# A gated block of local attention and GeGLU on one core: the instruction order is written by a list scheduler, the first token block goes in two halves, and TensorE gets warm-up matmuls

## The chip, the cores and the metric

The kernel runs on one core of a Trainium2 chip. Its time is that of one execution on the device in microseconds, and the median of several executions is what kernels are compared by. A core has five engines that run side by side, each through its own list of instructions in the order of that list: TensorE (PE, matmuls), VectorE (DVE), ScalarE (ACT), GpSimd (POOL) and SyncE (SP), which here only issues DMAs. An instruction that waits for another engine holds up everything behind it in its own list.

## The reference

The input x is 2048 tokens of 512 features, in bfloat16. After a layer norm without weights two branches start: an attention with 32 heads of 16 features, in which each token looks at itself and at seven earlier tokens two apart (offsets 0, 2, ..., 14), and a GeGLU feed-forward with 1792 hidden features. The output is x plus the attention branch times the silu of the feed-forward branch.

```python
def _A_ref(x, wqkv, wo):
    B, S, D = x.shape
    H = 32; Dh = D // H
    W, dil = 8, 2
    qkv = (lambda x, *d: x.transpose(*d))((x @ wqkv).reshape(B, S, 3, H, Dh), 2, 0, 3, 1, 4)
    q, k, v = qkv[0], qkv[1], qkv[2]
    scale = Dh ** -0.5
    pos = jnp.arange(S)
    off = jnp.arange(W) * dil
    idx = pos[:, None] - off[None, :]
    mask = idx >= 0
    ...
    logits = jnp.einsum("bhsd,bhswd->bhsw", q, kg) * scale
    logits = jnp.where(mask[None, None, :, :], logits, -1e9)
    attn = _softmax(logits, axis=-1)
    o = jnp.einsum("bhsw,bhswd->bhsd", attn, vg)
    return (lambda x, *d: x.transpose(*d))(o, 0, 2, 1, 3).reshape(B, S, D) @ wo
...
def _B_ref(x, w_gate, w_up, w_down):
    g = jnp.einsum("bsd,df->bsf", x, w_gate)
    u = jnp.einsum("bsd,df->bsf", x, w_up)
    h = _gelu(g) * u
    return jnp.einsum("bsf,fd->bsd", h, w_down)

x = A_x
xn = _layernorm(x, axis=-1)
s = _A_ref(xn, A_wqkv, A_wo)
g = _silu(_B_ref(xn, B_w_gate, B_w_up, B_w_down))
return x + s * g
```

## The kernel before

Tokens are taken in four blocks of 512 (`NJ`, index `j`), each of four tiles of 128 (`TPB`). All of x, the normalised and transposed x (`xnT`), the keys (`k_sb`) and all weights lie in on-chip memory. The weights come in one DMA each; `wqkv_sb` shares its place with the hidden activations `hT`.

*Layer norm.* `ln_stats` (from L194) has VectorE compute mean and variance of the four tiles of a block, and GpSimd `1/sqrt(var + eps)` by an add and a power (L200, L203). `ln_norm` (L210) normalises a tile on VectorE; `ln_transpose` transposes it by four TensorE matmuls (L224) and VectorE copies the result out of PSUM into `xnT` (L225).

*QKV.* `qkv_group` makes 128 of the 1536 output features for a block by four matmuls over 512 tokens (L416), and ScalarE copies them from PSUM: queries (L428), keys (L430), and values (L435), which are also written to DRAM (`vT_dram`, L436). There are twelve such groups a block.

*Attention* of a block (`queue_scores`, `queue_values`). VectorE multiplies the queries by shifted windows of the keys (L247, eight products of 128x2048); TensorE adds them up by head with a 0/1 matrix into `L_ps` (L260, 16 matmuls for each half of the window offsets); ScalarE takes the exponential (L273); TensorE sums over the window (L291), VectorE takes the reciprocal (L299), TensorE spreads it back (L307) and ScalarE copies it (L315). VectorE then normalises and multiplies the weights by shifted values (L342, eight products), which `load_values` has fetched from `vT_dram` in two halves of four DMAs (L408); TensorE adds the products up into `O_ps` (L357, 16 matmuls a half) and ScalarE copies them out (L364).

*Feed-forward.* `ffn_pair` makes 128 hidden features: four matmuls for the gate (L450), gelu on ScalarE (L459), four for up (L465), and VectorE's product into `hT` (L475). There are 14 pairs a block. `out_tile` makes 128 tokens of output: the attention's projection (`s_ps`, four matmuls, L484), the down projection (`y_ps`, 14 matmuls, L495), silu on ScalarE (L505), two multiply-adds on VectorE (L509, L510) and the store (L512).

*PSUM.* Four buffers (`psf`) serve the groups of QKV, gate, up, s and y in turn; two (`psa`) the transposes, `L_ps`, sums and spreads; one (`pso`) `O_ps`.

*What sets the order.* It is written out when the kernel is built: the loops at the end emit QKV for blocks 0 to 3, then for each block its 14 pairs and its four output tiles. The layer norm of block j+1 is emitted at fixed places among the groups of block j. Attention is put between by rough clocks of three engines (`clk`): after each group `pump_dve` emits products from one queue in order as long as they fit before a given time, `pump_pe` and `pump_act` emit reductions and exponentials whose time has come. ScalarE's table loads (for gelu, exp, silu; plain copies need none) are in no clock. The first four tiles of x and all later x come on SyncE's queue, `wqkv` on ScalarE's; the other weights follow on SyncE's after the values of blocks 0, 1 and 2.

## Time and profile before

| | us |
|---|---|
| median of three executions | 259.02 (258.78 to 261.68) |
| profiled execution, its own time | 258.46 |
| its span, first to last instruction | 256.4 |
| TensorE busy | 228.1 (89%) |
| VectorE busy | 158.8 (62%) |
| ScalarE busy | 107.2 (42%) |
| GpSimd busy | 11.2 (4%) |
| granted TensorE clock, mean | 0.996 |

The span is the part of the execution between the first and the last instruction of the kernel; the rest of the time lies around it. Busy time of TensorE is the union of its matmuls from start to (modelled) end; matmuls overlap, so the mean duration of one (379 ns) is longer than the distance from one to the next. In the views below a line stands for the instructions of one source line; "idle before" or an entry in square brackets is the time in which the engine stood idle just before, and what released it.

### The profile page before, as it was taken

The numbers are of one execution on the slowest core, as the hardware profiler recorded it, in microseconds if no ns is written. First come the engines' busy times: TensorE is split into PE (matmuls) and PEld (weight loads), VectorE is DVE, ScalarE is ACT, GpSimd is POOL, SyncE is SP. The second block draws the span as 40 slices with busy tenths as digits, with TensorE's granted clock in tenths as the row PEclk, the third lists the DMA queues.
The fourth block names the chain that finished last, engine by engine and source line by source line (L and its number), as shares of the span: only waits on it lengthen the run. The fifth ranks groups of instructions, "written<-read, shape, count | busy, mean of one in ns | idle before, by whom it ended". The sixth has DMA issues, their size and how long they took to land.

```text
span 256.4 us, 3342 instructions
## 1 busy us (share of the span) xinstructions
PE 228.1 (89%) x1296; PEld 100.0 (39%) x1296; DVE 158.8 (62%) x228; ACT 107.2 (42%) x157; POOL 11.2 (4%) x46
## 2 busy tenths in 40 slices
PE   0069979798999998999779999999999999999993
PEld 0034433333344443434234444444444444444441
DVE  2464758789987988999869742239953134344131
ACT  2006644545576477444664433143444105334110
POOL 6104010100000000000000000000000000000000
PEclk9999999999999999999999999999999999999998
DMA  6900289995778600377003400100000010000001
GB/s 211 348 14 0 83 296 210 293 295 140 216 243 210 115 3 0 82 163 147 26 1 86 84 0 3 41 23 18 3 0 1 20 43 20 0 0 3 20 20 41
DMA packets 20511, 22.58 MB, mean 88 GB/s; under 512 B 1296, under 2 KB 19472, under 8 KB 20496
## 3 DMA queue, kind: packets, MB, share of 16 engines
q1 hardware_dynamic: 18912, 20.80, 31.1%
q10 hardware_dynamic: 1584, 1.57, 2.0%
q8 instruction: 10, 0.16, 0.3%
q14 instruction: 5, 0.04, 0.1%
HBM read 18.17 MB, written 4.19 MB: 87 GB/s over the span
## 4 chain that ended last, share of the span: by engine, by line
PE 77%; DVE 13%; ACT 3%; DMA 2%; POOL 1%; issue 1%; SPq 0%; POOLq 0%; ACTq 0%
PE y_ps L495 19%; PE g_ps L450 18%; PE u_ps L465 18%; PE qkv_ps L416 8%; PE s_ps L484 6%; DVE prod L247 5%; PE O_ps L357 3%; PE tr_ps L224 3%; DVE stats L196 2%; DMA x_sb<-in_A_x_dram 2%; DVE xnT L225 2%; PE L_ps L260 2%; DVE xn_t L210 2%; POOL rstd L203 1%; ACT L273 1%
## 5 line engine op out<-in xcount | busy, mean ns | idle before, releaser
L465 PE MATMUL u_ps<-xnT,wu_sb 128*128 128x512 bf16 x224 | 57.5, 379 | 0.0
L450 PE MATMUL g_ps<-xnT,wg_sb 128*128 128x512 bf16 x224 | 57.5, 379 | 0.0
L475 DVE TENSOR_TENSOR hT<-gl,u_ps 128x512 bf16<-128x512 bf16 x56 | 38.2, 684 | 30.8 <-PE u_ps L465 24.7
L459 ACT ACTIVATE gl<-g_ps 128x512 bf16<-128x512 f32 x56 | 33.2, 597 | 45.8 <-PE g_ps L450 45.5
L495 PE MATMUL y_ps<-wd_sb,hT 128*128 128x512 bf16 x224 | 51.0, 379 | 0.0
L416 PE MATMUL qkv_ps<-xnT,wqkv_sb 128*128 128x512 bf16 x192 | 45.7, 386 | 0.5 <-DVE xnT L225 0.5
L342 DVE TENSOR_TENSOR pv<-attn,v_arr 128x2048 bf16<-128x2048 bf16 x32 | 38.3, 1218 | 0.9 <-PE O_ps L357 0.8
L247 DVE TENSOR_TENSOR prod<-q_sb,k_sb 128x2048 bf16<-128x2048 bf16 x32 | 37.9, 1216 | 0.0
L509 DVE TENSOR_TENSOR sg<-sil,s_ps 128x512 bf16<-128x512 bf16 x16 | 11.0, 686 | 37.1 <-ACT sil L505 37.1
L495 PEld LDWEIGHTS <-hT 128*128 128x128 bf16 x224 | 21.9, 98 | 26.4
L465 PEld LDWEIGHTS <-wu_sb 128*128 128x128 bf16 x224 | 21.5, 98 | 26.7 <-issue 1.6
L450 PEld LDWEIGHTS <-wg_sb 128*128 128x128 bf16 x224 | 21.4, 98 | 26.5 <-issue 1.7
L505 ACT ACTIVATE sil<-y_ps 128x512 bf16<-128x512 f32 x16 | 9.6, 597 | 46.9 <-PE y_ps L495 46.9
L416 PEld LDWEIGHTS <-wqkv_sb 128*128 128x128 bf16 x192 | 18.1, 100 | 22.0 <-issue 4.2
L224 PE MATMUL tr_ps<-ident,xn_t 128*128 128x128 bf16 x64 | 7.2, 243 | 19.7 <-DVE xn_t L210 19.7
L428 ACT ACTIVATE q_sb<-qkv_ps 128x512 bf16<-128x512 f32 x16 | 9.6, 598 | 19.7 <-PE qkv_ps L416 19.7
L484 PE MATMUL s_ps<-wo_sb,o_sb 128*128 128x512 bf16 x64 | 16.5, 379 | 0.0
L430 ACT ACTIVATE k_sb<-qkv_ps 128x512 bf16<-128x512 f32 x16 | 9.6, 597 | 12.1 <-PE qkv_ps L416 11.9
L224 PEld LDWEIGHTS <-xn_t 128*128 128x128 bf16 x64 | 4.3, 106 | 25.7 <-DVE xn_t L210 25.0
L196 DVE BATCH_NORM_STATS2 stats<-x_sb 128x6 f32<-128x512 bf16 x16 | 10.7, 671 | 5.8 <-DMA x_sb<-in_A_x_dram 5.8
L435 ACT ACTIVATE vst<-qkv_ps 128x512 bf16<-128x512 f32 x16 | 9.6, 598 | 9.1 <-PE qkv_ps L416 5.4
L225 DVE COPY xnT<-tr_ps 128x512 bf16<-128x512 bf16 x16 | 6.8, 424 | 10.4 <-PE tr_ps L224 10.4
(44 smaller groups left out, 105.8 us busy)
## 6 DMA issues: line engine op xcount, KB each, us to landing
v_arr<-vT_dram SPq DMA_DIRECT2D x24, 260.0 KB, 5.4
vT_dram<-vst SPq DMA_DIRECT2D x16, 128.0 KB, 3.3
out_dram<-sg SPq DMA_DIRECT2D x16, 128.0 KB, 1.7
wg_sb<-in_B_w_gate_dram SPq DMA_DIRECT2D x1, 1792.0 KB, 9.1
wu_sb<-in_B_w_up_dram SPq DMA_DIRECT2D x1, 1792.0 KB, 10.1
wd_sb<-in_B_w_down_dram SPq DMA_DIRECT2D x1, 1792.0 KB, 9.0
wqkv_sb<-in_A_wqkv_dram ACTq DMA_DIRECT2D x3, 512.0 KB, 6.0
x_sb<-in_A_x_dram SPq DMA_DIRECT2D x3, 512.0 KB, 8.1
```

The lines of the kernel that those rows point to most:

```text
L196: nc.vector.bn_stats(out=stats[:, t, :], in_=x_sb[:, t, :])
L224: nc.tensor.transpose(tr_ps[:, c * P : (c + 1) * P], xn_t[:, c * P : (c + 1) * P], ident[:])
L225: nc.vector.tensor_copy(out=xnT[:, :, t * P : (t + 1) * P], in_=tr_ps[:].rearrange("p (c n) -> p c n", c=NC),)
L247: nc.vector.tensor_tensor(out=prod[:], in0=st["q"][:, c, :].unsqueeze(1).to_broadcast([P, 4, TQ]), in1=kwin, op=ALU.mult,)
L342: nc.vector.tensor_tensor(out=pv[:], in0=st["attn"][:, w2, :].unsqueeze(1).to_broadcast([P, 4, TQ]), in1=st["v"][half][:, 4 * (g % 2) : 4 ...
L416: nc.tensor.matmul(ps[:], lhsT=wqkv_sb[:, dk, fo * P : (fo + 1) * P], rhs=xnT[:, dk, j * TQ : (j + 1) * TQ], start=(dk == 0), stop=(dk == ...
L450: nc.tensor.matmul(g_ps[:], lhsT=wg_sb[:, dk, fc * P : (fc + 1) * P], rhs=xnT[:, dk, j * TQ : (j + 1) * TQ], start=(dk == 0), stop=(dk == ...
L459: nc.scalar.activation(out=gl[:], in_=g_ps[:], func=AF.Gelu_apprx_tanh)
L465: nc.tensor.matmul(u_ps[:], lhsT=wu_sb[:, dk, fc * P : (fc + 1) * P], rhs=xnT[:, dk, j * TQ : (j + 1) * TQ], start=(dk == 0), stop=(dk == ...
L475: nc.vector.tensor_tensor(out=hT[:, fc, :], in0=gl[:], in1=u_ps[:], op=ALU.mult)
L484: nc.tensor.matmul(s_ps[:], lhsT=st["o"][:, c, tt * P : (tt + 1) * P], rhs=wo_sb[:, c, :], start=(c == 0), stop=(c == NC - 1),)
L495: nc.tensor.matmul(y_ps[:], lhsT=hT[:, fc, tt * P : (tt + 1) * P], rhs=wd_sb[:, fc, :], start=(fc == 0), stop=(fc == NF - 1),)
```

## The change

Each piece of work (the matmuls of a group, a copy, a product, a DMA issue) becomes a `Task` with an engine, a duration, the tasks it needs, a priority, the buffers it takes and frees, and, on ScalarE, the function whose table it needs. `Order.run` then emits tasks one at a time: of all that can start, the one with the earliest start, then the lowest priority number, then the first one added. The QKV groups, feed-forward pairs and output tiles keep their order among each other (`add_main` chains them); everything else is placed by the model. The priority numbers are about -1 for layer norm, -2 for the feed-forward's multiply, -1.8 for the output's, and 1 to 4.5 for attention, by block. The durations are constants in the file. A table load is counted as 1.28.

The start is also changed. Tiles 0 and 2 of x are issued on SyncE's queue, 1 and 3 on ScalarE's, and `wqkv` on SyncE's behind them. Twelve matmuls on a tile of zeros are put at the head of TensorE's list. The first block's layer norm runs in two halves of two tiles: the square root is taken on ScalarE and the reciprocal on VectorE instead of the power on GpSimd, and of each two transposed tiles ScalarE copies one. The first block's QKV matmuls run over 256 tokens, first half for four groups, then the second half. Later blocks keep the power on GpSimd. The gate's and other weights are still issued on SyncE's queue after the values of blocks 0, 1 and 2 are stored, with a lower priority than the loads of v. The last output tile is computed, gated and stored in two halves of 256 columns.

Number and shape of buffers stay, except for the small new tiles, and what is computed stays.

```diff
--- before.py
+++ after.py
@@ -22,8 +22,101 @@
 EPS = 1e-5
...
-MM_COL = 0.075
+MM = 0.216
+COL16 = 1.1
+TR = 0.28
+PROD = 1.14
+HMUL = 0.6
+STATS = 0.8
+NORM = 0.36
+TRCOPY = 0.36
+ACT1 = 0.62
+ACT2 = 1.06
+TABLE = 1.28
+HOP = 0.2
...
+class Order:
...
+    def add(self, eng, dur, fn, deps=(), prio=0.0, takes=(), frees=(), func=None, opens=None, closes=None):
...
+    def ready(self, t):
+        start = self.clock.get(t.eng, 0.0)
+        for d, lat in t.deps:
+            if isinstance(d, float):
+                start = max(start, d)
+                continue
+            if d.end is None:
+                return None
+            start = max(start, d.end + (lat if d.eng != t.eng else 0.0))
+        if t.opens is not None and self.open.get(t.eng) not in (None, t.opens):
+            return None
+        for ring, key in t.takes:
+            n = len(self.taken[ring]) - self.bufs[ring]
+            if n >= 0:
+                at = self.freed.get((ring, self.taken[ring][n]))
+                if at is None:
+                    return None
+                start = max(start, at)
+        return start
+    def run(self):
+        left = list(self.tasks)
+        while left:
+            best = None
+            for t in left:
+                s = self.ready(t)
+                if s is None:
+                    continue
+                k = (round(s, 3), t.prio, t.seq)
+                if best is None or k < best[0]:
+                    best = (k, t, s)
+            assert best is not None, "no task can start"
+            _, t, s = best
+            left.remove(t)
+            dur = t.dur
+            if t.func is not None and t.func != self.table:
+                dur += TABLE
+                self.table = t.func
+            for ring, key in t.takes:
+                self.taken[ring].append(key)
+            if t.opens is not None:
+                self.open[t.eng] = t.opens
+            if t.closes is not None:
+                self.open[t.eng] = None
+            t.end = s + dur
+            self.clock[t.eng] = t.end
+            for r in t.frees:
+                self.freed[r] = t.end + HOP
+            t.fn()
+        return max(self.clock.values())
...
@@ -81,9 +184,10 @@
     wqkv_v = A_wqkv.rearrange("(k p) n -> p k n", p=P)
     for t in range(TPB):
-        nc.sync.dma_start(out=x_sb[:, t, :], in_=x2d[t * P : (t + 1) * P, :])
+        eng = nc.sync if t % 2 == 0 else nc.scalar
+        eng.dma_start(out=x_sb[:, t, :], in_=x2d[t * P : (t + 1) * P, :])
     for i in range(3):
-        nc.scalar.dma_start(
+        nc.sync.dma_start(
             out=wqkv_sb[:, :, i * D : (i + 1) * D], in_=wqkv_v[:, :, i * D : (i + 1) * D]
         )
     for j in range(1, NJ):
...
+    x_there = [3.2, 3.5, 3.8, 4.1] + [9.5] * 4 + [11.5] * 4 + [13.5] * 4
+    w_there = [6.0, 7.0, 8.0]
+    warm = cpool.tile([P, TQ], BF16, name="warm")
+    nc.vector.memset(warm[:], 0.0)
+    eps_sb = cpool.tile([P, 1], F32, name="eps_sb")
+    nc.vector.memset(eps_sb[:], EPS)
+    first = cpool.tile([P, 1], F32, name="first")
+    nc.scalar.activation(out=first[:], in_=eps_sb[:], func=AF.Sqrt)
+    order.table = "sqrt"
...
+    warm_ps = psa.tile([P, TQ], F32, name="warm_ps", tag="a")
+    for _ in range(12):
+        nc.tensor.matmul(warm_ps[:], lhsT=warm[:, 0:P], rhs=warm[:], start=True, stop=True)
+    order.clock["pe"] = 5.6
...
+        def rstd_act(t0, n, deps):
...
+            a = add("act", 0.25, sq, deps=deps, prio=prio, func="sqrt")
+            return add("dve", 0.08, rec, deps=[a], prio=prio - 0.01)
...
+        def rstd_pool(t0, n, deps):
...
+            return add("pool", 1.4, fn, deps=deps, prio=prio)
...
+        def norm(t, dep):
...
+            return add("dve", NORM, fn, deps=[dep], prio=prio, takes=[("xn", t)])
...
+        def transpose(t, dep, on_act):
...
+                if on_act:
+                    nc.scalar.activation(out=o, in_=i, func=AF.Copy)
+                else:
+                    nc.vector.tensor_copy(out=o, in_=i)
...
+            a = add("pe", TR, fn, deps=[dep], prio=-1.0, takes=[("a", ("tr", t))], frees=[("xn", t)])
+            copied[t] = add(
+                "act" if on_act else "dve", ACT1 if on_act else TRCOPY, copy, deps=[a],
+                prio=prio - 0.02, frees=[("a", ("tr", t))],
+            )
...
+        if j == 0:
+            for half in range(2):
+                pair = list(ts)[2 * half : 2 * half + 2]
+                r = rstd_act(pair[0], 2, [stat(t) for t in pair])
+                for t in pair:
+                    transpose(t, norm(t, r), on_act=t % 2 == 0)
+        else:
+            r = rstd_pool(ts[0], TPB, [stat(t) for t in ts])
+            for t in ts:
+                transpose(t, norm(t, r), on_act=False)
...
+    def add_main(dur, fn, deps=(), takes=(), frees=(), prio=0.0):
+        main[0] = add("pe", dur, fn, deps=[main[0], *deps], prio=prio, takes=takes, frees=frees)
+        return main[0]
...
+    def qkv(j):
+        for which in range(3):
+            mms = []
+            if j == 0:
+                for half in range(2):
+                    for c in range(NC):
+                        ts = (2 * half, 2 * half + 1)
+                        mms.append(
+                            add_main(
+                                2 * MM,
+                                lambda c=c, half=half, which=which: qkv_mm(
+                                    0, which, c, half * TQ // 2, (half + 1) * TQ // 2
+                                ),
+                                deps=[copied[t] for t in ts] + [(w_there[which], 0.0)],
+                                takes=[("f", ("qkv", 0, which, c))] if half == 0 else [],
+                            )
+                        )
+                mms = mms[NC:]
+            else:
+                for c in range(NC):
+                    mms.append(
+                        add_main(
+                            4 * MM,
+                            lambda c=c, which=which: qkv_mm(j, which, c, 0, TQ),
+                            deps=[copied[t] for t in range(j * TPB, (j + 1) * TPB)],
+                            takes=[("f", ("qkv", j, which, c))],
+                        )
+                    )
...
+                    st = add("sp", 0.6, store, deps=[e], prio=-1.0, frees=[])
+                    v_stored[j] = add(("dma", j, c), 2.6, lambda: None, deps=[(st, 0.0)], frees=[("vst", (j, c))])
...
+        if j < 3:
+            add("sp", 1.0, weights, deps=[v_stored[j]], prio=2.0)
...
+    def load_values(j, half):
...
+        issue = add("sp", 2.2, fn, deps=[v_stored[j]], prio=0.0, takes=[("va", (j, half))])
+        v_ready[j, half] = add(("dma", "va", j, half), 6.0, lambda: None, deps=[(issue, 0.0)])
...
+            ps = []
+            for c in range(NC):
+                key = ("S", j, w2)
+                ps.append(
+                    add(
+                        "dve", PROD, lambda c=c, product=product: product(c),
+                        deps=[q_ready[j], k_ready[j], *ps[-1:]], prio=prio,
+                        takes=[("pr", (*key, c))], opens=key, closes=key if c == NC - 1 else None,
+                        frees=[("q", j)] if w2 == 1 and c == NC - 1 else [],
+                    )
+                )
+            r = add(
+                "pe", COL16, reduce, deps=[ps[-1]], prio=-0.5, takes=[("a", ("L", j, w2))],
+                frees=[("pr", ("S", j, w2, c)) for c in range(NC)],
+            )
+            exps.append(
+                add(
+                    "act", ACT1, expo, deps=[r], prio=-0.6, func="exp",
+                    takes=[("attn", j)] if w2 == 0 else [], frees=[("a", ("L", j, w2))],
+                )
+            )
...
+            ps = []
+            key = ("V", j, half)
+            for i in range(4):
+                last = i == 3
+                ps.append(
+                    add(
+                        "dve", PROD,
+                        lambda i=i, half=half, product=product: product(2 * half + i // 2, i % 2),
+                        deps=[n, v_ready[j, half], *ps[-1:]], prio=prio,
+                        takes=[("pr", (*key, i))], opens=key, closes=key if last else None,
+                        frees=([("va", (j, half))] if last else [])
+                        + ([("attn", j)] if last and half == 1 else []),
                     )
...
+        g = add_main(4 * MM, lambda: matmuls(wg_sb, "g_ps"), takes=[("f", ("g", j, fc))])
+        a = add(
+            "act", ACT1, gelu, deps=[g], prio=-0.5, func="gelu", takes=[("gl", (j, fc))],
+            frees=[("f", ("g", j, fc))],
+        )
+        u = add_main(4 * MM, lambda: matmuls(wu_sb, "u_ps"), takes=[("f", ("u", j, fc))])
+        h_ready[j, fc] = add(
+            "dve", HMUL, mult, deps=[a, u], prio=-2.0, takes=[("h", j)] if fc == 0 else [],
+            frees=[("f", ("u", j, fc)), ("gl", (j, fc))],
+        )
...
+    def out_tile(j, tt, parts):
...
+        add_main(
+            4 * MM, s_mms, deps=[o_ready[j]], takes=[("f", ("s", t))], frees=[("o", j)] if last else [],
+        )
+        n = D // parts
+        for p in range(parts):
+            cs = slice(p * n, (p + 1) * n)
+            end = p == parts - 1
+            for lo, hi in ((0, NF // 2), (NF // 2, NF)):
+                y = add_main(
+                    (hi - lo) * MM / parts,
+                    lambda lo=lo, hi=hi, cs=cs: y_mms(lo, hi, cs),
+                    deps=[h_ready[j, hi - 1]],
+                    takes=[("f", ("y", t))] if lo == 0 and p == 0 else [],
+                    frees=[("h", j)] if last and hi == NF and end else [],
+                )
+            a = add(
+                "act", ACT1 / parts + 0.1 * (parts - 1), lambda cs=cs: silu(cs), deps=[y], prio=-0.5, func="silu",
+                takes=[("sg", t)] if p == 0 else [], frees=[("f", ("y", t))] if end else [],
+            )
+            d = add(
+                "dve", 1.05 / parts, lambda cs=cs: gate(cs), deps=[a], prio=-1.8,
+                frees=[("f", ("s", t))] if end else [],
+            )
+            st = add("sp", 0.6, lambda cs=cs: store(cs), deps=[d], prio=-0.5)
+            add(("dma", "out", t, p), 2.0, lambda: None, deps=[(st, 0.0)], frees=[("sg", t)] if end else [])
+    for j in range(NJ):
+        layer_norm(j)
+    for j in range(NJ):
+        qkv(j)
+    order.freed["h", "wqkv"] = 0.0
+    for j in range(NJ):
         for half in range(2):
...
+            ffn_pair(j, fc)
         for tt in range(TPB):
-            out_tile(j, hT, tt)
-            attn_state[j]["out"] = tt == TPB - 1
-            pump_act(clk["pe"])
-            pump_pe(clk["pe"])
+            out_tile(j, tt, 2 if j == NJ - 1 and tt == TPB - 1 else 1)
+    order.run()
```

662 lines of the change are left out of this document (321 added, 341 removed).

## The prediction

> **What bounds the kernel now.** I read the head of the page first, then the span cut into stretches, then TensorE's waits, then the timeline of the start and the end.
>
> ```profile
> span 256.4 us, 3342 instructions
> PE 228.1 (89%) x1296; PEld 100.0 (39%) x1296; DVE 158.8 (62%) x228; ACT 107.2 (42%) x157; POOL 11.2 (4%) x46
> ```
>
> TensorE is the engine to explain: 89% busy, VectorE 62%, ScalarE 42%. The profiled execution took 258.46 us, so 2.06 us lie outside the span; it is 0.56 below the median of 259.02. The sum below is made against 258.46.
>
> Next the stretches: start, QKV with layer norm, first feed-forward block, its output tiles and a little more, the rest, the end. Columns: us, then busy us and instructions of each engine.
>
> ```profile
> 0.00:16.81 16.81, 2.43 (x17) 1.48 (x18) 6.52 (x17) 1.28 (x1) 5.43 (x25) 1.00 0.70 218
> 16.81:76.00 59.19, 53.31 (x345) 23.00 (x345) 45.77 (x75) 31.07 (x53) 5.76 (x21) 1.00 0.70 190
> 76.00:104.84 28.84, 28.14 (x176) 12.12 (x173) 25.58 (x31) 18.51 (x27) 0.00 (x0) 1.00 0.35 77
> 104.84:130.00 25.16, 22.30 (x154) 9.05 (x153) 21.71 (x26) 12.99 (x15) 0.00 (x0) 1.00 0.48 107
> 130.00:251.98 121.98, 121.95 (x612) 54.31 (x610) 58.15 (x81) 42.72 (x63) 0.00 (x0) 1.00 0.08 21
> 251.98:256.40 4.42, 0.00 (x0) 0.00 (x0) 1.11 (x2) 0.60 (x1) 0.00 (x0) 0.79 0.09 30
> ```
>
> From 130 us on TensorE has no gap: nothing but fewer or faster matmuls helps there. What an order can win lies ahead of 130 and in the last 4.42 us. Length less busy time gives 5.88, 0.70 and 2.86 us of idle TensorE in the three stretches from 16.81 to 130, and 14.4 before 16.81. Who it waits for:
>
> ```profile
> PE tr_ps L224 <- DVE xn_t L210: 19.7, 13, 11.3
> PE sum_ps L291 <- ACT attn L273: 3.6, 2, 2.9
> ```
>
> So there are two waits: the transposes of the layer norm (the first, 11.3 us, is the start; the rest are norms that come late among attention products on VectorE), and the softmax sums, which stand in TensorE's order ahead of an exponential that ScalarE has not done.
>
> **The start.** Columns: start, us, engine, line.
>
> ```profile
> 3.28 0.69 DVE L196 BATCH_NORM_STATS2 stats<-x_sb 128x6 f32<-128x512 bf16 x1 [3.28 <-DMA x_sb<-in_A_x_dram]
> 8.43 0.67 DVE L196 BATCH_NORM_STATS2 stats<-x_sb 128x6 f32<-128x512 bf16 x1
> 9.12 0.18 DVE L197 BATCH_NORM_AGGREGATE mv<-stats 128x2 f32<-128x6 f32 x1
> 9.80 1.04 POOL L203 TENSOR_TENSOR rstd<-rstd,mhalf 128x4 f32<-128x4 f32 x1
> 10.87 0.41 DVE L210 TENSOR_SCALAR xn_t<-x_sb,mv,rstd 128x512 bf16<-128x512 bf16 x1 [1.56 <-POOL rstd L203]
> 11.34 0.61 PE L224 MATMUL tr_ps<-ident,xn_t 128*128 128x128 bf16 x4 [11.34 <-DVE xn_t L210]
> 16.33 0.42 DVE L225 COPY xnT<-tr_ps 128x512 bf16<-128x512 bf16 x1 [0.70 <-PE tr_ps L224]
> 16.81 5.56 PE L416 MATMUL qkv_ps<-xnT,wqkv_sb 128*128 128x512 bf16 x20 [0.52 <-DVE xnT L225]
> 5.00:10.00 5.00, 0.00 (x0) 0.00 (x0) 2.52 (x6) 0.00 (x0) 0.76 (x4) 1.00 1.10 354
> ```
>
> The first tile of x is there at 3.28, the fourth is read at 8.43, because wqkv comes on the other queue meanwhile. Then GpSimd's power, and a serial walk of norm, transpose, copy over four tiles, up to 16.81.
>
> In the change the four tiles are issued first, two on each queue, and wqkv behind them. At the 354 GB/s of the last row a tile of 131 KB takes 0.37 us, so I put them at 3.3, 3.7, 4.0 and 4.4; each third of wqkv (0.52 MB) then takes 1.5, so they are there at about 5.9, 7.4 and 8.9, and the second block of x at 10.3. Two tiles of statistics at 0.87 (0.69 and 0.18) end at 5.0. The Sqrt on ScalarE has no row; its bounds are 0.1 and 0.60 (a 128x512 ACT, quoted below), and I take 0.25, since it has two columns, with 0.19 of handover (9.30 to 9.49, GpSimd's start behind the statistics). The tiny reciprocal I put at 0.18 (the aggregate's row), behind at most 0.4 of a third tile's statistics: 6.0. Two norms (0.41 each) end at 6.8, four transposes 0.61, a fourth tile's statistics (0.87) ahead of the copy, copy 0.42: 8.1, and with some 0.4 of handovers 8.5. Were the tiles as late as now, the second half could not start before about 12; were all waits short, 7.5. I take 8.5, and 0.5 of TensorE idle between the two halves. Halving the columns of the first block's matmuls costs nothing by the transposes, which with 128 columns go at 0.23 for four, weights included (below).
>
> The cold clock. The 20 matmuls at 16.81 take 5.56 where 20 x 0.216 (3.02 for 14, below) is 4.31: 1.25 us lost. The 12 matmuls on zeros run while nothing else could, at 0.46 each if five of those 20 were the slow ones ((5.56 - 15 x 0.216)/5), so 5.5 us from about 1 us on, and hold the first transpose (6.4) back by little. That they save the 1.25 no row shows; bounds 0 and 1.25, and I take the whole, since only some 2 us of transposes lie between. In the Trainium skill, "TensorE: Matmul & The Clock Gate" (Part 1 and Part 4) has a free-running window of about 3.4 us that must be busy, and says that transposes do not count as busy. By that rule it is a matter of phase whether 5 us of warm-up hold one whole window, and the sum would be 1.25 higher in the bad phase; no row here decides it.
>
> **TensorE's own work from the first QKV matmul on.**
>
> ```profile
> 155.68 3.02 PE y_ps L495 x14
> 80.46 0.98 PE O_ps L357 x16
> 81.44 0.97 PE u_ps L465 x4
> 82.41 0.86 PE g_ps L450 x4
> 22.20 0.39 PE L224 MATMUL tr_ps<-ident,xn_t 128*128 128x128 bf16 x4
> 22.43 1.89 PE L416 MATMUL qkv_ps<-xnT,wqkv_sb 128*128 128x512 bf16 x8
> 58.19 0.29 PE L291 MATMUL sum_ps<-attn,fold 128*32 128x128 bf16 x8
> 58.41 1.04 PE L416 MATMUL qkv_ps<-xnT,wqkv_sb 128*128 128x512 bf16 x4
> ```
>
> The loops give 192 + 448 + 64 + 224 = 928 large matmuls: x 0.2157 = 200.2. Sixteen attention reductions at 0.98, and 0.11 more on the group behind each (0.97 against 0.86): 17.4. Twelve tiles of transposes at 0.23 (22.20 to 22.43): 2.8. Four sums and four spreads at 0.22 (58.19 to 58.41): 1.8. Together 222.2. Before, the same stretch is 251.98 - 16.81 = 235.2, so 13.0 are lost in it: 9.5 idle, 1.25 cold, the other 2.2 the pipeline's drain ahead of each wait (the busy times count it).
>
> **What the new order leaves of these 13.0.** The planner takes at each step the task that can start first, and gives LayerNorm and the feed-forward's multiplies priority over attention. Next late after the transposes would be VectorE's load.
>
> ```profile
> 41.27 2.27 DVE prod L247 x2
> L475 DVE TENSOR_TENSOR hT<-gl,u_ps 128x512 bf16<-128x512 bf16 x56 | 38.2, 684 | 30.8 <-PE u_ps L465 24.7 <-ACT gl L459 4.2 <-ACT o_sb L364 1.5
> ```
>
> A product is 1.135, so a block's 16 are 18.2, with reciprocal and normalise some 20. A tile of layer norm is 0.87 + 0.41 + 0.42 = 1.7, so 20 for three blocks. From 10.3 on, layer norm, one block of attention and 14 multiplies of 0.68 are 50 us, so 60; TensorE gets to the first output tiles only at about 9 + 41.4 + 2.8 + 24.2 + 5 x 1.09 = 83. VectorE has 23 us to spare, and the second block's layer norm (statistics to 13.8, GpSimd 1.55 to 15.4, then 0.83 a tile to 18.7 and a little) is ahead of TensorE, which needs it at about 20: cover of 1 us, and its price if x is later by 2 is 1 us.
>
> With layer norm done at about 30 (10.3 + 20), block 0's attention (20) and block 1's scores (8 x 1.135 and a reciprocal) fill VectorE to the end of QKV near 60. So four of the eight exponentials come while ScalarE only copies, and four fall among gelu or silu. What that costs:
>
> ```profile
> 89.52 1.28 ACT L273 ACT_TABLE_LOAD   x1 [0.44 <-PE L_ps L260]
> 90.82 0.60 ACT L273 ACTIVATE attn<-L_ps 128x512 bf16<-128x512 f32 x1
> 91.43 1.28 ACT L459 ACT_TABLE_LOAD   x1
> 92.72 1.08 ACT L459 ACTIVATE gl<-g_ps 128x512 bf16<-128x512 f32 x2
> ```
>
> One exponential holds ScalarE for 3.20 us. TensorE runs three groups (2.59) past a gate before it needs that buffer again. A gelu that comes right behind the exponential ends 3.8 after its gate, 1.2 late; its multiply, behind a product of 1.13 on VectorE, can make that 2.2. In the row above it cost TensorE nothing (0.70 idle in the whole stretch, all of it at a sum). Bounds per exponential 0 and 2.2; I take 0.8, x 4 = 3.2. The sums' 3.6 us go, since the planner counts the table load (1.28 in it, 1.28 here) and issues them afterwards.
>
> In the Trainium skill, "ScalarE: Activation LUTs" (What ACT_TABLE_LOAD costs) adds a drain of 1.38 us to each load, 2.66 a switch. By that rule the exponentials would hold ScalarE 2.76 longer each, and the sum would be up to 11 higher. The trace disagrees: from the load's start to the exponential 1.30, from its end at 91.42 to the next load 0.01.
>
> **The end.**
>
> ```profile
> 251.99 0.60 ACT L505 ACTIVATE sil<-y_ps 128x512 bf16<-128x512 f32 x1 [3.29 <-PE y_ps L495]
> 252.62 0.69 DVE L509 TENSOR_TENSOR sg<-sil,s_ps 128x512 bf16<-128x512 bf16 x1 [2.74 <-ACT sil L505]
> 253.34 0.42 DVE L510 TENSOR_TENSOR sg<-sg,x_sb 128x512 bf16<-128x512 bf16 x1
> ```
>
> 1.71 of compute and 2.64 of store. Halved in columns the compute is between 0.86 and 1.71; I take 1.15, so 3.85 instead of 4.42.
>
> **Moved with no price.** Two of the first copies go to ScalarE, idle then. Memsets and table load stand where all engines wait for x. On SyncE's queue the gate's weights now come behind block 0's loads of v:
>
> ```profile
> 30.76 1.47 SPq L98 DMA_DIRECT2D wg_sb<-in_B_w_gate_dram  x1
> wg_sb<-in_B_w_gate_dram SPq DMA_DIRECT2D x1, 1792.0 KB, 9.1
> ```
>
> Block 0's v leaves TensorE some 8 us sooner and eight loads come in between, so I leave the issue near 31; with 9.1 to land it is there at 40, and needed near 60. Without that cover it would be the whole wait.
>
> **The sum:** 8.5 + 0.5 + 222.2 + 3.2 + 3.85 = 238.3 of span, + 2.06 = 240.4 us.
>
> **Rivals.**
>
> *Same waits in other places.* The order is fixed when the kernel is built, each engine keeps to it, and wherever a real duration differs from the planner's constants an engine waits at the head of its queue. For it: the constants leave out DMA traffic and queue depth. Against: they fit the rows (0.216 and 0.2157, 1.14 and 1.135, 1.28). If all 13.0 less the cold 1.25 come back in place of the 3.2, it is 240.4 + 8.6 = 249. Chance 0.22, spread over 244 to 253.8.
>
> *Late v, slower than before.*
>
> ```profile
> v_arr<-vT_dram SPq DMA_DIRECT2D x24, 260.0 KB, 5.4
> v_arr<-vT_dram SPq DMA_DIRECT2D x2, 255.0 KB, 10.6
> ```
>
> The planner counts 6.0 to landing. Products with v that are queued too early hold VectorE, and behind them the multiplies that empty PSUM. Three groups of 0.86 less the multiply's 0.68 give 1.9 of cover. With 10.6 at each of eight halves, 8 x (4.6 - 1.9) = 21.6: 262. It decides from 10.2 on, where 8 x 2.3 = 18 undo the gain; at 10.9 it is beyond 2% (264). Against it: the median of 24 out of 32 was 5.4, and the loads are issued long ahead of use. Chance 0.04 beyond 2%, and 0.08 for all that ends within 2%.
>
> *The change doesn't warm the clock, or the tiles come as late as now:* 241.7, or 3.5 more, 243.9; inside the first case.
>
> **How the numbers follow.** Forecast 0.66, from 236.5 (no stall left: 240.4 - 3.2 - 0.5 = 236.7) to 244. The part of the next case up to 249 has 0.14 of its 0.22, which makes 236.5 to 249 for 8 in 10. About 2% is what a measurement of this kernel can tell from no change: faster than 253.8 holds the first two cases, 0.88; within 0.08; slower 0.04.
>
> **What would show it.** First QKV matmul near 8.5 and its pace 0.216 from the first on; no wait of transposes behind norms past the start; sums without a wait; TensorE idle between first and last matmul near 4; the stretch from last matmul to end near 3.9. I am wrong if TensorE waits for ScalarE's gelu or VectorE's multiplies for more than 8 us, if v's DMA shows as a releaser of products, or if the first matmul comes after 12.

## The result and the profile after

The changed kernel takes 249.67 us (median of 248.14 to 252.04), the kernel before 260.06 beside it: a ratio of 0.958 (95% interval 0.947 to 0.968). It is faster by 4.2%, where 240.4 us and 7% were forecast, and its median lies 0.7 us above the range of 236.5 to 249. One of its four executions, 252.04 us, ran in a slower state of the chip and is not in the ratio; the other three have a median of 248.55, just inside the range. The profiled execution took 248.14 us, 1.84 of them outside its span.

The head of the page after, and the span in stretches: start, QKV, first feed-forward block, its output tiles and a little more, the rest, the end (us, then busy us of each engine, granted clock, DMA share, GB/s):

```profile
span 246.3 us, 3508 instructions
PE 231.6 (94%) x1370; PEld 107.5 (44%) x1370; DVE 157.3 (64%) x232; ACT 110.6 (45%) x164; POOL 10.9 (4%) x44
```

```profile
0.00:8.16 8.16, 5.35 (x21) 2.02 (x21) 4.65 (x15) 2.67 (x5) 4.17 (x23) 1.00 0.81 249
8.16:61.95 53.79, 52.48 (x416) 28.47 (x417) 51.13 (x84) 34.15 (x57) 6.77 (x21) 1.00 0.77 214
61.95:99.27 37.32, 32.30 (x206) 13.01 (x205) 29.89 (x35) 21.28 (x27) 0.00 (x0) 0.95 0.72 155
99.27:122.97 23.70, 22.45 (x147) 9.33 (x145) 23.44 (x28) 12.69 (x16) 0.00 (x0) 1.00 0.28 63
122.97:242.60 119.63, 119.07 (x586) 54.70 (x585) 47.48 (x72) 39.48 (x61) 0.00 (x0) 1.00 0.04 14
242.60:246.30 3.70, 0.00 (x0) 0.00 (x0) 0.71 (x2) 0.34 (x1) 0.00 (x0) 0.69 0.12 35
```

The start has shrunk from 16.81 to 8.16 us, the end from 4.42 to 3.70, and QKV has 1.3 us of idle TensorE where it had 5.9. One stretch got worse: the first feed-forward block has 5.0 us of idle TensorE where it had 0.7, and a granted clock of 0.95. Its waits, and the timelines of VectorE and TensorE:

```profile
DVE pv L605 <- DMA v_arr<-vT_dram: 7.4, 1, 7.4
PE u_ps L666 <- DVE hT L683: 4.5, 1, 4.5
```

```profile
71.82 1.23 DVE L605 TENSOR_TENSOR pv<-attn,v_arr 128x2048 bf16<-128x2048 bf16 x1 [7.40 <-DMA v_arr<-vT_dram]
```

```profile
68.21 1.03 PE L666 MATMUL g_ps<-xnT,wg_sb 128*128 128x512 bf16 x4
73.69 1.87 PE L666 MATMUL u_ps<-xnT,wu_sb 128*128 128x512 bf16 x4 [4.45 <-DVE hT L683]
75.35 1.71 PE L666 MATMUL g_ps<-xnT,wg_sb 128*128 128x512 bf16 x4
```

It is one event. VectorE has a product with the second half of block 1's values at the head of its list, and these values are not there. The multiply that empties PSUM stands behind it, so TensorE runs out of buffers at 69.07 (68.21 + 0.86) and stands until 73.69. Then the two next groups take 1.66 and 1.64 us in place of 0.86: the clock has gone down. With 0.47 us of a second wait at 78.3, the event costs 4.6 + 1.6 + 0.5 = 6.7 us.

Why the values are late is in SyncE's queue (start, time to issue) and in two pieces of the chain of waits:

```profile
45.46 0.45 SPq L446 DMA_DIRECT2D wu_sb<-in_B_w_up_dram  x1
46.07 2.91 SPq L434 DMA_DIRECT2D vT_dram<-vst  x4
49.02 8.54 SPq L451 DMA_DIRECT2D wo_sb<-in_A_wo_dram  x4
57.60 0.59 SPq L452 DMA_DIRECT2D wd_sb<-in_B_w_down_dram  x1
58.30 8.68 SPq L474 DMA_DIRECT2D v_arr<-vT_dram  x8
```

```profile
45.46 11.53 DMA wu_sb<-in_B_w_up_dram
61.77 9.93 DMA v_arr<-vT_dram
```

The longest wait of SyncE at `wo`, and how long `wd` took from issue to landing:

```profile
SPq L451 <- DMA wu_sb<-in_B_w_up_dram: 5.4, 1, 5.4
wd_sb<-in_B_w_down_dram SPq DMA_DIRECT2D x1, 1792.0 KB, 9.1
```

SyncE issues `wo` and `wd`, which TensorE first needs at 99.27, ahead of these values. The last of the four DMAs of `wo` waits until `wu` has landed (45.46 + 11.53 = 56.99). The values follow `wd`, which lands at 66.7 (57.60 + 9.1), and they land in the 5 us behind it, the last part at 71.7. On SyncE's queue, here and in the traces of all the other runs, DMAs landed in the order in which they were issued. The planner had counted 6.0 us.

### The profile page after: what moved, and what is told of

It reads as the page before. It is cut to its first block, busy times and chain, and to the rows that moved or that the text cites. A ratio compares the mean times of both kernels' runs of the same rounds, so it can differ in the third digit from the quotient of the medians.

```text
span 246.3 us, 3508 instructions
## 1 busy us (share of the span) xinstructions
PE 231.6 (94%) x1370; PEld 107.5 (44%) x1370; DVE 157.3 (64%) x232; ACT 110.6 (45%) x164; POOL 10.9 (4%) x44
## 4 chain that ended last, share of the span: by engine, by line
PE 55%; DVE 20%; DMA 16%; issue 4%; SPq 3%; ACT 1%; DVEq 0%; ACTq 0%
PE y_ps L720 15%; PE u_ps L666 14%; PE g_ps L666 14%; DVE prod L495 6%; DVE pv L605 6%; PE qkv_ps L368 5%; DMA wu_sb<-in_B_w_up_dram 5%; PE s_ps L708 4%; DMA v_arr<-vT_dram 4%; DMA vT_dram<-vst 4%; DMA x_sb<-in_A_x_dram 3%; DVE hT L683 3%; SPq L474 2%; DVE stats L277 2%; DVE sg L736 1%
## 5 line engine op out<-in xcount | busy, mean ns | idle before, releaser
L666 PE MATMUL u_ps<-xnT,wu_sb 128*128 128x512 bf16 x224 | 58.4, 384 | 4.9 <-DVE hT L683 4.5
L720 PE MATMUL y_ps<-wd_sb,hT 128*128 128x512 bf16 (+1 forms) x238 | 51.6, 367 | 0.5 <-ACT sil L732 0.5
L368 PE MATMUL qkv_ps<-xnT,wqkv_sb 128*128 128x512 bf16 (+1 forms) x240 | 44.9, 337 | 0.8 <-ACT rstd L284 0.8
L736 DVE TENSOR_TENSOR sg<-sil,s_ps 128x512 bf16<-128x512 bf16 (+1 forms) x17 | 11.1, 655 | 36.7 <-ACT sil L732 36.7
L720 PEld LDWEIGHTS <-hT 128*128 128x128 bf16 x238 | 23.0, 98 | 26.5 <-issue 1.8
L368 PEld LDWEIGHTS <-wqkv_sb 128*128 128x128 bf16 x240 | 22.4, 98 | 17.3 <-issue 2.7
L732 ACT ACTIVATE sil<-y_ps 128x512 bf16<-128x512 f32 (+1 forms) x17 | 9.7, 572 | 41.9 <-PE y_ps L720 41.9
L630 ACT ACTIVATE o_sb<-O_ps 128x1024 bf16<-128x1024 f32 x8 | 8.2, 1024 | 5.7 <-PE O_ps L619 5.1
L708 PEld LDWEIGHTS <-o_sb 128*128 128x128 bf16 x64 | 6.1, 98 | 7.1
L619 PE MATMUL O_ps<-pv,fold 128*32 128x512 bf16 x128 | 8.7, 382 | 0.5 <-DVE pv L605 0.5
## 6 DMA issues: line engine op xcount, KB each, us to landing
wu_sb<-in_B_w_up_dram SPq DMA_DIRECT2D x1, 1792.0 KB, 11.5
```

The source lines that it names most:

```text
L368: nc.tensor.matmul(tiles["qkv", j, fo][:, lo:hi], lhsT=wqkv_sb[:, dk, fo * P : (fo + 1) * P], rhs=xnT[:, dk, j * TQ + lo : j * TQ + hi], s ...
L666: nc.tensor.matmul(ps[:], lhsT=w[:, dk, fc * P : (fc + 1) * P], rhs=xnT[:, dk, j * TQ : (j + 1) * TQ], start=(dk == 0), stop=(dk == NC - 1),)
L708: nc.tensor.matmul(s_ps[:], lhsT=tiles["o", j][:, c, tt * P : (tt + 1) * P], rhs=wo_sb[:, c, :], start=(c == 0), stop=(c == NC - 1),)
L720: nc.tensor.matmul(tiles["y", t][:, cs], lhsT=tiles["h", j][:, fc, tt * P : (tt + 1) * P], rhs=wd_sb[:, fc, cs], start=(fc == 0), stop=(fc ...
L732: nc.scalar.activation(out=tiles["sil", t][:, cs], in_=tiles["y", t][:, cs], func=AF.Silu)
L736: nc.vector.tensor_tensor(out=sg[:, cs], in0=tiles["sil", t][:, cs], in1=tiles["s", t][:, cs], op=ALU.mult)
```

## The experiments

Theory A: TensorE lost these 6.7 us because a product with v was queued before its v had landed, and the order on SyncE's queue made it land late. Theory B: the DMA engines are full from 24 to 86 us, so some product waits whatever the order. All ratios are against the kernel before on the same chip.

**e1.** The planner is told that v lands later; VectorE's order changes with it.

```diff
-        v_ready[j, half] = add(("dma", "va", j, half), 6.0, lambda: None, deps=[(issue, 0.0)])
+        v_ready[j, half] = add(("dma", "va", j, half), 18.0, lambda: None, deps=[(issue, 0.0)])
```

> Only the planner's constant for the landing of v changes, 6.0 to 18.0; the DMAs keep their order up to block 2. Theory A (TensorE lost about 7 us at 68 to 78 because a product with v was queued on VectorE before its v had landed, and the multiplies behind it empty PSUM): four score products now stand ahead of the first product with v(1,1), v lands near 72 as before, VectorE's wait of 7.4 us goes, and the time is 241 to 243. Theory B (the DMA engines are full from 24 to 86 us, so some product waits whatever the order): the wait comes back at v(2,0) or v(2,1), 3 us or more, and the time stays at 246 to 250.

244.05 us, ratio 0.932 (0.928 to 0.936). No product waits for a DMA any more, although v(1,1) lands at 72.6, no sooner than before: eight score products now stand ahead of the first one with it (four were expected). That is A, and not B. It ends 1 us above the expected 241 to 243 for another reason, in TensorE's timeline:

```profile
8.30 1.89 PE L368 MATMUL qkv_ps<-xnT,wqkv_sb 128*128 128x256 bf16 x8 [1.15 <-DMA wqkv_sb<-in_A_wqkv_dram]
118.48 1.02 PE L666 MATMUL g_ps<-xnT,wg_sb 128*128 128x512 bf16 x4 [1.88 <-ACT gl L676]
120.19 1.02 PE L666 MATMUL u_ps<-xnT,wu_sb 128*128 128x512 bf16 x4 [0.69 <-ACT gl L676]
```

In this order an exponential stands between two gelus at 115.9 us, right behind a silu, with three table loads around it (112.7, 114.6, 116.5), and TensorE pays 2.6 us for it (1.88 + 0.69). And in this execution the first QKV matmuls were slow in spite of the warm-up (8 in 1.89 us; 1.03 in the changed kernel).

**e2.** `wo` and `wd` are issued behind the loads of v(1,1).

```diff
-        if j < 3:
+        late_weights[j] = weights
+        if j < 2:
             add("sp", 1.0, weights, deps=[v_stored[j]], prio=2.0)
...
             load_values(j, half)
+    add("sp", 1.0, late_weights[2], deps=[v_ready[1, 1]], prio=2.0)
```

> Only the issue of wo and wd moves, from ahead of the loads of v(1,1) and v(2,0) on SyncE's queue to behind them and the stores of block 3. Theory A, with the cause on SyncE's queue: v(1,1) is issued at 56 to 58 in place of 58 to 62 and with nothing large ahead of it lands by 65 in place of 72; VectorE's wait falls from 7.4 to under 1.5 us, the time is 241 to 243. Theory B: the load of wu and the stores still fill the engines, v(1,1) lands at 69 or later, and the time is 245 or more; or wd lands after 99 and the first output tile waits.

242.76 us, ratio 0.929 (0.926 to 0.933), profiled span 239.7. SyncE's queue and VectorE:

```profile
54.38 7.50 SPq L477 DMA_DIRECT2D v_arr<-vT_dram  x8
69.39 0.64 SPq L454 DMA_DIRECT2D wd_sb<-in_B_w_down_dram  x1
```

```profile
60.73 5.77 DVE L608 TENSOR_TENSOR pv<-attn,v_arr 128x2048 bf16<-128x2048 bf16 x5
```

The fifth product of the row is the one that waited; now it runs on without a gap, though with little to spare: the last part of v(1,1) lands at 64.5, and the product starts at 65.27. Moving five DMAs (`wo` and `wd`) on one queue gives 6.6 us of span, as much as the event cost; the lists of instructions of all the computing engines are the same as in the changed kernel, one by one. B falls. From 24 to 86 us the DMA engines are as full as they were and move as much (the changed kernel, then e2; the last columns are granted clock, DMA share, GB/s), and no product waits:

```profile
24.00:86.00 62.00, 57.08 (x390) 23.97 (x388) 54.37 (x65) 36.08 (x56) 3.63 (x13) 0.97 0.98 242
24.00:86.00 62.00, 61.53 (x429) 26.44 (x435) 61.77 (x75) 41.19 (x63) 3.63 (x13) 1.00 0.98 243
```

**e3 and e4.** Two other ways to get the weights out of the way: `wg` and `wu` right behind x, or `wo` and `wd` from GpSimd's queue.

```diff
+    nc.sync.dma_start(out=wg_sb[:], in_=B_w_gate.rearrange("(k p) n -> p k n", p=P))
+    nc.sync.dma_start(out=wu_sb[:], in_=B_w_up.rearrange("(k p) n -> p k n", p=P))
     x_there = [3.2, 3.5, 3.8, 4.1] + [9.5] * 4 + [11.5] * 4 + [13.5] * 4
...
         def weights():
-            if j == 0:
-                nc.sync.dma_start(out=wg_sb[:], in_=B_w_gate.rearrange("(k p) n -> p k n", p=P))
-            elif j == 1:
-                nc.sync.dma_start(out=wu_sb[:], in_=B_w_up.rearrange("(k p) n -> p k n", p=P))
-            elif j == 2:
+            if j == 2:
```

> wg and wu are issued right behind x at about 7 us, when the DMA engines are idle from 13 to 24, instead of behind the values of blocks 0 and 1. Theory A: v(1,1) still stands behind wo and wd on SyncE's queue, but these are no longer held up by wu: issue at 56, landing at 62 to 66, wait under 2 us, time 241 to 243. Theory B: 3.7 of the 16.6 MB leave the full stretch, so it agrees; it is told apart by the two other runs. If the early 3.7 MB hold up the first stores of v (20.8 us), block 0's v lands a few us later, at a cost of nothing.

```diff
-                    nc.sync.dma_start(out=wo_sb[32 * e : 32 * (e + 1), :, :], in_=wo_v[e])
-                nc.sync.dma_start(out=wd_sb[:], in_=B_w_down.rearrange("(k p) n -> p k n", p=P))
+                    nc.gpsimd.dma_start(out=wo_sb[32 * e : 32 * (e + 1), :, :], in_=wo_v[e])
+                nc.gpsimd.dma_start(out=wd_sb[:], in_=B_w_down.rearrange("(k p) n -> p k n", p=P))
```

> wo and wd are issued from GpSimd's queue, without a wait, so near 42 us. Theory A in the form that SyncE's queue is what held v up (it took 8.5 us to issue wo, since wu was in front): v(1,1) is issued at 56 at the latest and lands by 64; wait under 1.5 us, time 241 to 243. Theory B: the same bytes go through the same engines, wu and v(1,0) land 5 us or more later and v(1,1) at 69 or later; time 245 or more.

e3: 246.7 us, 0.940 (0.935 to 0.946); e4: 248.09, 0.949 (0.944 to 0.954). Both miss what A expected. VectorE's wait in e3, then a piece of the chain, the time that `wu` took to land, and TensorE's wait in e4:

```profile
68.64 1.23 DVE L603 TENSOR_TENSOR pv<-attn,v_arr 128x2048 bf16<-128x2048 bf16 x1 [3.56 <-DMA v_arr<-vT_dram]
```

```profile
49.67 18.40 DMA vT_dram<-vst
```

```profile
wu_sb<-in_B_w_up_dram SPq DMA_DIRECT2D x1, 1792.0 KB, 19.2
```

```profile
68.82 1.02 PE L666 MATMUL g_ps<-xnT,wg_sb 128*128 128x512 bf16 x4 [4.22 <-ACT vst L388]
```

In e3 `wo` issued in 2.6 us, no longer held by `wu`, and v(1,1) was issued at 54.11 instead of 58.30, as early as in e2 (54.38). But `wd` was still in front of it and landed at 63.4 (53.07 + 10.3); v(1,1) landed 5.1 us behind it, as in the changed kernel (66.7 and 71.7), and came 3.6 us late. So the bytes ahead decide, and not the time of issue. In e4 SyncE's queue was free of `wo` and `wd`, but not of `wu`, which was issued at 48.56 with 2.4 MB from GpSimd's queue under way. `wu` took 19.2 us in place of 11.5 and landed at 67.8, and a store of values issued behind it took 18.4 and landed at 68.07 (the same store took 11.1 in the changed kernel). ScalarE could not get a buffer back, and TensorE waited 4.2 us; VectorE waited 6.0 for v(1,1) besides. (This is e4's slowest execution; the median is 1.9 us lower.) So A holds in a narrower form: not the time that SyncE needs to issue, but the bytes of weights that are under way ahead of an urgent load or store. From another queue they did it too, by way of `wu`.

The next runs are made on top of e2, where this event is gone, to price the terms of the start and the end.

**e5.** One warm-up matmul in place of twelve.

```diff
-    for _ in range(12):
+    for _ in range(1):
```

> Run on top of the kernel of e2 (wo and wd late). Eleven of the twelve warm-up matmuls are left out. By the prediction's term (the whole 1.25 us is saved by them) the first 20 or so QKV matmuls run at half pace again and the end of the last matmul moves by 1.0 to 1.7 us; the span of e2 was 239.7, so 240.7 to 241.4. By the rival that they do not warm the clock, since a phase decides, the first eight half-width matmuls take the same 1.05 us as in e2.

Span 239.5, 241.15 us, ratio 0.923 (0.917 to 0.929): nothing lost. TensorE's timeline of e2, then of e5:

```profile
7.92 1.05 PE L368 MATMUL qkv_ps<-xnT,wqkv_sb 128*128 128x256 bf16 x8 [0.83 <-DMA wqkv_sb<-in_A_wqkv_dram]
18.43 0.40 PE L325 MATMUL tr_ps<-ident,xn_t 128*128 128x128 bf16 x4 [2.47 <-DVE xn_t L309]
```

```profile
8.14 1.86 PE L368 MATMUL qkv_ps<-xnT,wqkv_sb 128*128 128x256 bf16 x8 [0.61 <-DVE rstd L290]
18.22 0.40 PE L325 MATMUL tr_ps<-ident,xn_t 128*128 128x128 bf16 x4 [0.57 <-DVE xn_t L309]
```

The warm-up does warm the clock (1.05 against 1.86 for eight), but a wait takes back what it gave: near 18 us both stand until the second block's layer norm is there. The expected 1.0 to 1.7 us did not come.

**e6.** The last tile in one piece (`parts` 1 for all tiles).

> Run on top of the kernel of e2. The last output tile is computed and stored in one piece. The prediction had the split save 0.57 us at the end. The trace of the changed kernel has TensorE idle inside the split tile (0.47 us on the silu of the first half, and the drain ahead of it), so I now expect last matmul to end 4.4 in place of 3.7 us but the last matmul 0.6 earlier: the sum of both within 0.2 us of e2.

Span 239.5, 241.51 us, ratio 0.926 (0.921 to 0.932): the same as e2. The split shortens the end, but stops TensorE inside it, as in the changed kernel:

```profile
241.59 0.93 PE L720 MATMUL y_ps<-wd_sb,hT 128*128 128x256 bf16 x7 [0.47 <-ACT sil L732]
```

**e7 and e8.** The whole start undone, and only the queues of x and `wqkv` undone.

```diff
-        eng = nc.sync if t % 2 == 0 else nc.scalar
-        eng.dma_start(out=x_sb[:, t, :], in_=x2d[t * P : (t + 1) * P, :])
+        nc.sync.dma_start(out=x_sb[:, t, :], in_=x2d[t * P : (t + 1) * P, :])
     for i in range(3):
-        nc.sync.dma_start(
+        nc.scalar.dma_start(
...
-    x_there = [3.2, 3.5, 3.8, 4.1] + [9.5] * 4 + [11.5] * 4 + [13.5] * 4
+    x_there = [3.3, 5.5, 7.6, 8.4] + [9.5] * 4 + [11.5] * 4 + [13.5] * 4
```

e7 also has one warm-up matmul, the power on GpSimd for all blocks, and no halves.

> Run on top of the kernel of e2. The whole start is undone: x on SyncE's queue and wqkv on ScalarE's, the power on GpSimd, no halves, no warm-up matmuls; the scheduler's order stays. By the prediction's terms the first QKV matmul comes at 16.8 in place of 7.9 and runs cold (1.25), so the span is 239.7 + 8.9 + 1.25 = 249.9, or a little less, since VectorE's and the DMA queues' later work has been waiting less. By a rival that DMA or VectorE set the first 90 us (both near full from 24 on), part of the start is given back: the span is 245 or less.

> Run on top of the kernel of e2. Only the issue of x and wqkv at the start is as before (x on one queue, wqkv on the other), with the planner told the arrivals of the page of before; halves, Sqrt and warm-up stay. If the early tiles are what moves the start, the fourth tile is there at 8.4 again, the second half starts at 11 to 12, and the first QKV matmul at 9 to 10: 3 to 4 us later than e2. If halves and Sqrt do most of it, it is within 1.5 us of e2.

e7: span 251.7, 253.32 us, ratio 0.970 (0.966 to 0.974). e8: span 242.8, 245.09 us, 0.938 (0.932 to 0.944).

```profile
16.40 6.41 PE L366 MATMUL qkv_ps<-xnT,wqkv_sb 128*128 128x512 bf16 x20 [0.87 <-DVE xnT L331]
```

The whole start undone costs 12.0 us of span, 1.8 more than expected. Of this, 8.5 is the later first matmul (16.40 against 7.92) and 2.1 its cold clock (6.41 where 20 x 0.2157 is 4.31). But e7 also has 2.7 us of waits of TensorE for gelu and silu that e2 does not have, so the 12.0 is not the start alone. The scheduler's order and the late `wd` by themselves make the kernel 3% faster. With the old queues of x the span is 3.1 longer; e8's first 16 matmuls ran at half pace (3.40 us where 1.9 would do), so not all of this need be the queues.

**e9 to e12.** The changed kernel again, and the second block's layer norm. e10 tells the planner later arrivals of x; e11 issues the second block of x ahead of two thirds of `wqkv` and gives the last tile's halves a PSUM buffer each; e12 is e11 without the warm-up.

```diff
-    x_there = [3.2, 3.5, 3.8, 4.1] + [9.5] * 4 + [11.5] * 4 + [13.5] * 4
-    w_there = [6.0, 7.0, 8.0]
+    load_wqkv(0)
+    for j in range(1, NJ):
+        if j == 2:
+            load_wqkv(1)
+            load_wqkv(2)
...
+    x_there = [3.2, 3.5, 3.8, 4.1] + [9.5] * 4 + [15.5] * 4 + [15.5] * 4
+    w_there = [7.5, 11.0, 12.5]
...
-            if lo == 0 and cs.start == 0:
-                tiles["y", t] = psf.tile([P, D], F32, name="y_ps", tag="f")
+            if lo == 0:
+                tiles["y", t, cs.start] = psf.tile([P, D], F32, name="y_ps", tag="f")
```

> The changed kernel itself, on the chip of the three other runs, so that they are compared with it side by side. VectorE's wait for v(1,1) is in it again (5 to 9 us), the time is 247 to 252.

> Run on top of the kernel of e2 (wo and wd late). Only the planner's arrival times of x are changed, to 12.0 for the second block and 15.5 for the third and fourth. Theory D (TensorE waits near 18 us for the second block's layer norm; VectorE's order with four statistics of the third block ahead of the second block's norms is part of it): with two of them gone from in front the norms start 1 to 1.6 us earlier, the wait of 2.5 us falls to about 1, span 238.3 to 239. Rival: the wait is set by the arrival of x alone (12.4 us), and stays above 2 us.

> Run on top of the kernel of e2. The second block of x is issued ahead of the second and third part of wqkv, the planner is told 9.5 for it and 15.5 for the rest, and the two halves of the last output tile get a PSUM buffer each. Theory D: the second block is there at 9 to 10, the wait near 18 us goes, the last half tile no longer waits 0.47 for silu: 239.7 - 2.5 - 0.6 = 236.6 of span. Rival: keys' or values' weights come later than the matmuls that need them (11 to 13 us) and TensorE waits there instead, 1 us or more.

> The kernel of e11 without eleven of the twelve warm-up matmuls. In e5 leaving them out cost nothing, since the slow first matmuls were absorbed by the wait at 18 us (2.47 with them, 0.57 without). Theory D: with that wait gone the cold start is paid in full, 1.2 to 1.9 us more than e11. Rival: warm-up is worth nothing in any case: within 0.4 us of e11.

e9: 248.56 us, 0.952 (0.947 to 0.957), with VectorE's wait for v of 7.8 us in it. e10: 241.84 us, 0.926 (0.919 to 0.933), span 239.6. e11: 238.53 us, 0.914 (0.910 to 0.918), span 236.8. e12: 240.4 us, 0.919 (0.914 to 0.925), span 239.2. TensorE in e11, then in e12:

```profile
8.14 1.03 PE L373 MATMUL qkv_ps<-xnT,wqkv_sb 128*128 128x256 bf16 x8 [0.82 <-ACT rstd L289]
15.57 0.61 PE L330 MATMUL tr_ps<-ident,xn_t 128*128 128x128 bf16 x8
229.86 3.22 PE L728 MATMUL y_ps<-wd_sb,hT 128*128 128x256 bf16 x28
```

```profile
8.13 1.89 PE L373 MATMUL qkv_ps<-xnT,wqkv_sb 128*128 128x256 bf16 x8 [0.75 <-DMA wqkv_sb<-in_A_wqkv_dram]
```

With x there in time the transposes come at 15.57 without a wait, the last tile's 28 matmuls run through, and the span is 2.9 us under e2 (3.1 expected). Now the warm-up pays: without it the span is 2.4 us longer (the second block's transposes come at 18.00 in place of 15.57), and the median 1.9. e10 met only half of what was expected: the wait fell from 2.47 to 0.65, but the span stayed; its first gate came 1.0 us sooner, its last matmul ended 0.2 sooner. About half of the difference went into a wait for a gelu that e2 does not have, 0.39 and some drain ahead of it; the rest is in pieces too small to name:

```profile
82.92 1.02 PE L669 MATMUL g_ps<-xnT,wg_sb 128*128 128x512 bf16 x4 [0.39 <-ACT gl L679]
```

e11 beats the changed kernel by 4% on the same chip.

## Why the prediction was wrong

Faster was right, the size was not. The terms of the sum, as forecast, in the changed kernel, and in e11:

| us | forecast | changed | e11 |
|---|---|---|---|
| first QKV matmul | 8.5 | 8.16 | 8.14 |
| TensorE waits between the halves | 0.5 | 0 | 0 |
| TensorE's own work | 222.2 | as e11 | 223.1 |
| what is lost in that stretch | 3.2 | 11.3 | 1.9 |
| end | 3.85 | 3.70 | 3.72 |
| outside the span | 2.06 | 1.84 | 2.45 |

(Own work in e11: 233.08 - 8.14 = 224.9, less three waits of 0.69, 0.39 and 0.29 and some 0.17 of drain for each. Lost in the changed kernel: 242.60 - 8.16 = 234.4, less 223.1. Of these 11.3, 6.7 are the event and 3.0 four more waits: 1.31, 0.73, 0.50, 0.47. Of the 0.9 by which the forecast of TensorE's own work is too low, some 0.46 (2 x 0.23) is two tiles of transposes: it counted twelve tiles, and the two of the first block's second half come on top.)

*The step that failed* is the third rival's dismissal, that the loads of v "are issued long ahead of use", with the 5.4 us to landing taken from the kernel before. Of that kernel it is true. Its v(1,1), issued and first used (start, us, engine):

```profile
73.91 2.37 SPq L408 DMA_DIRECT2D v_arr<-vT_dram  x4
106.08 2.35 DVE L342 TENSOR_TENSOR pv<-attn,v_arr 128x2048 bf16<-128x2048 bf16 x2
```

That is 32 us. In the changed kernel v(1,1) is issued at 58.30, and VectorE is ready for it at 64.42 (71.82 - 7.40): 6.1 us, since the scheduler starts each task as early as its model allows, and the model says 6.0. Its four parts take 9.7 to 10.4 us each to land, because `wd` is ahead of them. The prediction followed one weight past one queue, `wg`, and not `wu`, `wo` and `wd`. It had the sign before it: the 10.6 us in its own row are loads of block 0 issued right behind `wg` (at 30.76). With everything 8 us earlier, 242 GB/s go through the DMA engines from 24 to 86 us (15.0 MB) where it was 214 (13.3 MB) in the kernel before, and the stores of v land after 9.1 us in the median where it was 3.3. The prediction's sign that it is wrong, v's DMA as a releaser of products, is what the trace shows.

The rival was right in kind and wrong in number: one half of eight was late, not all, and the cover was 2.8 us (7.4 of wait less 4.6 of idle TensorE) where it took 1.9. So its chances, 0.04 and 0.08, were for the wrong event: all halves late. One late half belonged into the likeliest case, as 3 to 7 us.

*A term that was missing*: the price of a stall is more than the stall. After 4.6 us idle TensorE took 3.3 us for two groups that need 1.7. The granted clock fell to 0.50 for 3.4 us (73.3 to 76.7); e1, e3, e4, e8 and e9 show falls of the same length, each worth some 1.7 us of TensorE. In the kernel before, the stall of 2.86 us was followed by a group at full pace:

```profile
129.63 0.24 PE L291 MATMUL sum_ps<-attn,fold 128*32 128x128 bf16 x4 [2.86 <-ACT attn L273]
129.80 1.04 PE L450 MATMUL g_ps<-xnT,wg_sb 128*128 128x512 bf16 x4
```

The Trainium skill, "TensorE: Matmul & The Clock Gate" (Part 1), has the clock fall after an idle window of about 3.4 us; these two rows agree, but other runs do not, if one goes by the length of a single wait. e3 shows a fall with no wait longer than 1.33 us near it, and e4 one behind a wait of 2.27 near 18 us (the clock is the third figure from the end):

```profile
75.12 0.58 PE L617 MATMUL O_ps<-pv,fold 128*32 128x512 bf16 x4 [1.33 <-DVE pv L603]
75.63 1.89 PE L664 MATMUL u_ps<-xnT,wu_sb 128*128 128x512 bf16 x4
77.31 1.68 PE L664 MATMUL g_ps<-xnT,wg_sb 128*128 128x512 bf16 x4
```

```profile
20.00:21.00 1.00, 1.00 (x7) 0.67 (x6) 0.71 (x3) 0.00 (x0) 0.92 (x2) 0.50 0.00 0
```

What decides when the clock falls stays open. With the same warm-up, the first matmuls were at full pace in the changed kernel and slow in e1 and e8. That the page's window is free-running would fit this; but in e1 and e8 TensorE also stood a little longer ahead of the first matmul (1.15 and 0.90 us, against 0.82), and the runs do not tell the two apart.

*The warm-up* was taken at the whole 1.25 us. It does warm the clock (1.05 against 1.86 for eight), but in e5 the gain ended in the wait for the second block's layer norm, and only in e11 was it paid out, as 1.9 to 2.4 us. The 1.25 itself is a little high: the 5.56 us run to the end of the last of the 20 matmuls, and to the next start (22.20) it is 5.39, which leaves 1.08.

*The second block's layer norm* was given 1 us of cover, with a price of 1 us if x came 2 us later. x came at 11.47 (10.3 forecast), VectorE did four statistics of the third block first, and TensorE waited 1.31 us. That is right in kind and too small in size: by the prediction's price, x being 1.2 us later would have cost 0.2.

```profile
17.51 0.40 PE L325 MATMUL tr_ps<-ident,xn_t 128*128 128x128 bf16 x4 [1.31 <-DVE xn_t L309]
```

*Exponentials among gelu and silu*: 0.8 each was too much for the changed kernel, where no wait of TensorE is put down to them; e1 shows 2.6 us for one in a bad place, a little over the upper bound of 2.2. So the bound was 0.4 too low, and the value a guess. Their table loads cost what the prediction took (ScalarE in the changed kernel, 1.30 from load to exponential, no drain):

```profile
85.12 1.28 ACT L520 ACT_TABLE_LOAD   x1 [0.50 <-PE L_ps L508]
86.42 0.60 ACT L520 ACTIVATE attn<-L_ps 128x512 bf16<-128x512 f32 x1
```

*The start* (8.5) and *the end* (3.85) were right as numbers. The end's saving of 0.57 was not real: what the split saves behind the last matmul it costs ahead of it (e6). *The rival of the same waits in other places* gave 249, almost the result, and for a wrong reason: the waits were not spread over the order, one DMA made most of them.

## What to carry to other kernels

When a change makes the start earlier or the loop shorter, go through each DMA queue in its new order and ask, for every load that is soon needed, how many bytes stand in front of it: a landing time taken from the slower kernel no longer holds. Put weights that are needed late behind the loads that are needed soon; another queue for them did not help here (e4). A scheduler that starts each task as early as its model allows leaves no slack for an error of the model, so give it landing times from a trace under load. A wait that it doesn't know of costs TensorE the wait, and can cost a slow clock after it: 3.4 us at half pace behind 4.45 us of waiting, none behind 2.86 in the kernel before.

## What was not expected of the hardware

- An issue can wait for other DMAs of its queue: in this program SyncE's DMAs take eight completion semaphores in turn, and each waits for the eighth before it. So the four issues of `wo`, behind `wu`, held SyncE for 8.54 us, 5.4 of them until `wu` had landed, and 2.6 us where `wu` was long there (e3).
- A store of 128 KB took 18.4 us to land behind 1.8 MB of `wu` on its own queue, with 2.4 MB of weights under way from GpSimd's (e4). The same store took 11.1 in the changed kernel, and in the kernel before the median of such stores was 3.3.
- The granted clock in the profile shows a fall, but not the cold start. In the kernel before it is 1.00 at 16.81 us, where the first ten matmuls took 3.40 us (2.2 at full pace); in the changed kernel it is 0.83 in the 10 us with the stall:

```profile
70.00:80.00 10.00, 5.84 (x31) 2.10 (x31) 8.18 (x10) 2.22 (x3) 0.00 (x0) 0.83 1.12 242
```
